# Attention of six blocks in 13 visits of TensorE with two units each, where 36 visits took one unit each

## The chip, the cores and the metric

The kernel runs on one core of a Trainium2 chip. The metric is the device time of one execution in microseconds (us). Three runs of the kernel before took 731.62, 733.33 and 733.63 us, a median of 733.33 us. A difference of less than about 0.3% (2.2 us) can't be told from none here.

## The reference

Two stages follow each other. The first is attention in chunks of 32 queries, each of which sees 8 memory keys, 16 keys to its left, its own 32 and 8 to its right; the second is a gated network with a norm ahead of it.

```python
q, k, v: (4 batches, 8 heads, 768 positions, 64)
for c in range(768 // 32):
    k_full = [mem_k, k[c*32-16 : c*32+32+8]]     # v_full likewise
    a = softmax(q_c @ k_full.T / 8)
    out[c] = a @ v_full
x  = out as (3072 tokens, 512)
xn = x / sqrt(mean(x*x) + 1e-6) * rms_g
y  = (silu(xn @ w_gate) * (xn @ w_val)) @ w_out   # 512 -> 1536 -> 512
```

## The kernel before

**Units and blocks.** The 3072 tokens are worked in eight blocks of 384. The attention of one block is four units, each of two heads (32 units in all, numbered 0 to 31). A unit runs through these steps: load q and k (`load_qk`) and v (`load_v`), transpose q and k on VectorE (`stage_t`, which ScalarE ends with two small copies inside k's tile), twelve score matmuls `s` (`stage_s`, L318), the maximum and the subtraction (`stage_m`: `mx` L330, `pe` L336), the exponential on ScalarE (`stage_e`, L341), three transposes of the weights on TensorE (`stage_p`: `pT`, L348), their copy out of PSUM in two halves, the first on ScalarE and the second on VectorE (`stage_c`, lines L227 and L230), twelve output matmuls `o` (`stage_o`, L368), and the division into the tile `x` (`stage_r`: L382, L386, L391). After a block's fourth unit `stage_n` norms `x`.

**The network.** Each block is worked through f = 0 to 11, twelve tiles of 128 hidden columns. For each f TensorE does twelve matmuls into `pg`, twelve into `pv` (L561, 384 columns each), and nine into the three `po` banks (L599, 512 columns) for the f before it. Every product is three matmuls on high and low parts in fp32r. From `pg` and `pv` ScalarE and VectorE make `t`, `hh` and `hl` (L568, L572, L575, L227, L584), which `po` takes 6 us later. At a block's end the next block's `x` is transposed on TensorE (`xT`, L440) and split into `xh` and `xl`.

**Order.** Up to 158 us a hand-written list (`ORDER`) sets everything: the attention of blocks 0 and 1 (units 0 to 7), the network of block 1, and the first five f of block 0. From there the main loop runs over six segments: block 0 from f = 5 on, then blocks 2 to 7. The gaps of a segment are numbered: after `pg` of its f-th tile comes gap 2f, after `pv` gap 2f+1 (counted from the segment's first f). In some of these gaps TensorE visits the attention of the next block. On TensorE the order of the program is kept. On the other engines a scheduler sets the order when the program is built, and each engine then works its own list strictly in that order; the attention steps have the higher priority.

**Visits before.** A block's attention takes seven steps, of which six have matmuls: visit n does `pT` of unit n-1, `s` of unit n and `o` of unit n-2. So what `o` needs was copied out of PSUM a visit earlier. All units of blocks 2 to 7 use one set of tiles: one for transposed q and weights (`qp`, in the place `A`), one for k and v (`kv`, in the place `B`), one landing tile for q (`qn`) and one for k (`kn`).

**PSUM.** `pg`, `pv` and the three `po` have one bank each. The other three banks are a ring (`psa`) which `pT`, `s`, `o`, `xT` and the scratch of the norm take in turn: a tile that is fourth in the ring waits until the first has been read out.

Of the kernel before, what the change touches and what calls it, by code (L numbers as in the profile page):

```python
# [8 lines left out]
F32 = mybir.dt.float32  # L9
# [10 lines left out]
CH = 32  # L20
# [16 lines left out]

FIRST = (1, 3, 5, 7, 9, 10, 11)
GAPS = 4
FA, FC = 3, 5  # L40
# [27 lines left out]
def tile_kernel(ctx: ExitStack, tc: tile.TileContext, q, k, v, mem_k, mem_v,  # L68
# [32 lines left out]
    pts = [None] + [early.tile([P, NT, 4, 2, CH], F32, name=f"pt{i}") for i in (1, 2)]  # L101
    zero = const.tile([P, 64], F32, name="zero")

# [13 lines left out]
    NE = NG * 2  # L117
    late_kv = {}
    KW, VW = (NC + 1) * KC, NJ * 2 * (D + 1)

    def late_attention():

        t = p1.tile([P, NKT * HT], F32, name="qp", tag="A")
        n = NC * 2 * CH
        qbs[0] = t[:, 0:n].rearrange("p (c s q) -> p c s q", c=NC, s=2)
        pts[0] = t[:, n:].rearrange("p (i a s q) -> p i a s q", i=NT, a=4, s=2)
        nc.vector.memset(t, 0.0)
        t = p1.tile([P, KW + VW], F32, name="kv", tag="B")
        late_kv["kw"] = t[:, 0:KW].rearrange("p (c k) -> p c k", k=KC)
        late_kv["vw"] = t[:, KW:].rearrange("p (j h d) -> p j h d", j=NJ, h=2)  # L130
    units = [(b, hf, g) for b in range(B) for hf in range(2) for g in range(NG)]
    st = {}

    def which(u):

        return 1 + u % 2 if u < NE else 0

    def unit_tile(u, shape, tag, n):

        if u < NE:  # L140
            return early.tile(shape, F32, name=f"{tag}{u}", tag=f"{tag}{u % n}")
        if tag in late_kv:
            return late_kv[tag]
        return p1.tile(shape, F32, name=f"{tag}{u}", tag=tag)

    def load_qk(u):
        b, hf, g = units[u]
        h0 = 2 * g
        t0 = hf * HT
        d = st.setdefault(u, {})  # L150
        if u < NE:

            k0 = t0 - hf * CH
            for n, src, r0, rows in (("q", q, t0, HT), ("k", k, k0, HT + CH)):
                x = d[n] = early.tile([P, 8, D], F32, name=f"{n}f{u}", tag=f"{n}f{u % NG}")[0:rows // 4]
                nc.sync.dma_start(out=x.rearrange("p (h r) d -> p h (r d)", h=2),
                                  in_=src[b, h0:h0 + 2, r0:r0 + rows].rearrange("h (p r) d -> p h (r d)", r=4))
            return

        d["q"] = qn = p1.tile([P, NC, CH], F32, name=f"qn{u}", tag="qn")  # L160
# [107 lines left out]
    def stage_q0(u, e="a"):  # L268
        d = st[u]
        qb = qbs[which(u)]  # L270
        q4 = split4(d["tq"], HT)
# [11 lines left out]
    def stage_ta(u):  # L283
        d = st[u]
        qb = qbs[which(u)]
        for hh in range(2):
# [22 lines left out]
    def stage_s(u):  # L309
        d = st[u]  # L310
        qb = qbs[which(u)]
        s = psum_a(f"s{u}")
# [42 lines left out]
    def stage_ch(u, hh, e):  # L355
        r = slice(64 * hh, 64 * hh + 64)
        t4 = st[u]["t"][:, 0:HT].rearrange("p (i a q) -> p i a q", i=NT, q=CH)
        copy(e, pts[which(u)][r, :, :, hh, :], t4[r])

    def stage_o(u):  # L360
        d = st[u]
        pt = pts[which(u)]
        o = psum_a(f"o{u}") if u >= NG else psum_m(f"o{1 + u % 2}", f"o{u}")
# [37 lines left out]
    def stage_n0(x):  # L401
        ss = p2.tile([P, 2, NT], F32, name="ss", tag="ss")
        squares(x, 0, NG - 1, ss[:, 0])
        return ss
# [4 lines left out]
    def stage_ny(ss):  # L409
        sr = p2.tile([P, NT], F32, name="sr", tag="sr")  # L410
        nc.vector.scalar_tensor_tensor(out=sr, in0=ss[:, 0], scalar=DM * 1e-6, in1=ss[:, 1], op0=ALU.add, op1=ALU.add)
# [239 lines left out]
    for cp in range(2):  # L651
        nc.scalar.dma_start(out=memV[64 * cp:64 * cp + NM], in_=mem_v[0].rearrange("h m d -> m h d"))
    first = const.tile([P, 1], F32, name="first")
    nc.scalar.activation(first, zero[:, 0:1], AF.Exp)
# [32 lines left out]

    def attn_visits(blk, x):


        us = list(range(blk * NG, (blk + 1) * NG))
        for n in range(NG + 2):
            with tc.high_priority():
                if 1 <= n <= NG:
                    stage_p(us[n - 1])
                if n < NG:
                    u = us[n]
                    stage_s(u)
                if n >= 2:
                    stage_o(us[n - 2])  # L700
                    stage_r(us[n - 2], x)
                if n < NG:
                    stage_m(u)
                    stage_e(u)
                if 1 <= n <= NG:
                    stage_c(us[n - 1])
                if n < NG and u + 1 < len(units):
                    stage_t(u + 1)
            if n >= 2 and us[n - 2] + 1 < len(units):
                load_v(us[n - 2] + 1)  # L710
            if n < NG and u + 2 < len(units):
                load_qk(u + 2)
            yield
        with tc.high_priority():
            stage_n(x)
        yield

# [137 lines left out]
    xs = xs01[0]  # L855
    nxt = 2
    for sg, (blk, f0) in enumerate(segments):
        po = [psm_o(i) for i in range(NT)] if sg else sp["po", 0]
        todo = iter(())
        if nxt < NBLK:  # L860
            x = new_x()
            todo = attn_visits(nxt, x)
            nxt += 1
        last = sg == len(segments) - 1
        gaps = 2 * (NF - f0)
        when = [n * (gaps - GAPS) // (NG + 1) for n in range(NG + 2)] + [gaps - GAPS + 1]
        if sg == 0:
            when = FIRST

        def visit(gap):  # L870
            for _ in range(when.count(gap)):
                next(todo, None)
        for f in range(f0, NF):
# [18 lines left out]
            else:  # L892
                for _ in todo:
                    pass
                prev = moe_h(g, vv)
                xs = split_x(x, out_, lambda: moe_out(NF - 1, prev, po))
        if sg == 0:
# [31 lines left out]
```

## Time and profile before

| what | value |
|---|---|
| runs | 731.62, 733.33, 733.63 us |
| span of the profiled execution | 729.8 us (its own run time is not recorded with it; the span leaves out 3.5 us of the median) |
| VectorE, ScalarE, GpSimd busy | 52%, 39%, 5% of the span |
| matmuls `pg` and `pv` | 384 of each of six kinds, 337 to 346 ns each |
| matmuls `po` | 285 of each of three kinds, 393 to 399 ns each |
| `s` and `o` of blocks 2 to 7 | 576 matmul records each, 228 and 224 ns |
| one main-loop segment of a whole block | 86.3 us (`po` groups at 302.71 and 388.96 us) |

A matmul's duration includes its way through the array, and the next starts before it has ended: `pg` and `pv` start 0.17 us apart, `po` 0.23 us. What a step costs TensorE is therefore read from starts, not from durations. An fp32 matmul of the attention shows as two records, so twelve `s` are listed as x24.

### The profile page before, as it was taken

Reading aid. Unit: us, or ns where it says so; the run is one execution under the profiler, and the core shown is the slowest. Engines: PE = TensorE matmul, PEld = TensorE weight load, DVE = VectorE, ACT = ScalarE, POOL = GpSimd, SP = SyncE. Lnnn points to the kernel's source line nnn. Section 1 sums busy time; section 2 is a strip of 40 time slices with the busy share of each in tenths; the row PEclk is TensorE's granted clock in tenths of the full one; section 3 lists DMA queues with packets and bytes.
Section 4 is the critical chain, followed back from the end, with each engine's and each line's share of the span. In section 5 each row is a group of like instructions: output and inputs, shape, how many; then the busy total and the mean of one; then the engine's idle time right before and its main releaser. Section 6 shows DMA issues by size and latency. Waiting matters only on the chain.

```text
span 729.8 us, 13052 instructions
## 1 busy us (share of the span) xinstructions
PE 715.1 (98%) x5136; PEld 656.6 (90%) x5136; DVE 380.0 (52%) x725; ACT 287.8 (39%) x600; POOL 36.4 (5%) x143
## 2 busy tenths in 40 slices
PE   8889999999999999999999999999999999999997
PEld 7778999999989999899999999989998999999996
DVE  4888999865645443444535353445434543332222
ACT  4899676643452323422333232432234222341112
POOL 3300000001000000000000000000000000000000
PEclk8999999999999999999999999999999999999999
DMA  8994563414412320122212123021311210010001
GB/s 173 203 259 141 173 202 116 132 37 102 85 37 68 55 50 22 62 46 42 43 38 66 23 45 61 20 66 31 66 29 34 64 32 20 20 44 0 1 1 43
DMA packets 143173, 50.20 MB, mean 69 GB/s; under 512 B 126984, under 2 KB 134536, under 8 KB 143112
## 3 DMA queue, kind: packets, MB, share of 16 engines
q1 hardware_dynamic: 139832, 44.49, 26.6%
q10 hardware_dynamic: 3280, 4.88, 1.8%
q8 instruction: 40, 0.66, 0.4%
q14 instruction: 21, 0.17, 0.1%
HBM read 43.06 MB, written 6.29 MB: 68 GB/s over the span
## 4 chain that ended last, share of the span: by engine, by line
PE 92%; ACT 3%; DMA 3%; DVE 1%; issue 0%; POOL 0%; ACTq 0%; SPq 0%; POOLq 0%
PE pv L561 28%; PE po L599 28%; PE pg L561 27%; PE s L318 3%; PE o L368 3%; PE xT L440 1%; PE pT L348 1%; DMA ws<-in_moe_w_val_dram 1%; DMA memV<-in_mem_v_dram 1%; DMA vw<-in_v_dram 1%; ACT junk L398 0%; ACT ws L508 0%; ACT pt L227 0%; DMA kv<-in_v_dram 0%; ACT qb L227 0%
## 5 line engine op out<-in xcount | busy, mean ns | idle before, releaser
L561 PE MATMUL pv<-xh,wh_v 128*128 128x384 f32 x384 | 132.8, 346 | 0.0
L561 PE MATMUL pg<-xh,wh_g 128*128 128x384 f32 x384 | 129.7, 338 | 0.7 <-DVE t L572 0.7
L561 PE MATMUL pv<-xh,wl_v 128*128 128x384 f32 x384 | 129.5, 337 | 0.6 <-DVE wl_v L532 0.6
L561 PE MATMUL pg<-xh,wl_g 128*128 128x384 f32 x384 | 129.5, 337 | 0.0
L561 PE MATMUL pg<-xl,wh_g 128*128 128x384 f32 x384 | 129.3, 337 | 0.0
L561 PE MATMUL pv<-xl,wh_v 128*128 128x384 f32 x384 | 129.3, 337 | 0.0
L572 DVE SCALAR_TENSOR_TENSOR t<-t,pg 128x384 f32<-128x384 f32 x96 | 53.1, 553 | 138.6 <-ACT t L568 138.5
L227 ACT CAST hh<-t 128x384 fp32r<-128x384 f32 x95 | 48.7, 512 | 174.9 <-PE po L599 165.3
L599 PE MATMUL po<-wh_o,hh 128*128 128x512 f32 x285 | 113.8, 399 | 0.3
L599 PE MATMUL po<-wh_o,hl 128*128 128x512 f32 x285 | 113.1, 397 | 0.0
L599 PE MATMUL po<-wl_o,hh 128*128 128x512 f32 x285 | 112.1, 393 | 0.0
L584 DVE TENSOR_TENSOR hl<-t,hh 128x384 fp32r<-128x384 f32 x95 | 52.9, 557 | 100.7 <-ACT hh L227 95.7
L568 ACT ACTIVATE t<-pg 128x384 f32<-128x384 f32 x96 | 47.2, 492 | 135.9 <-PE pg L561 130.8
L575 DVE TENSOR_TENSOR t<-t,pv 128x384 f32<-128x384 f32 x95 | 52.5, 552 | 64.9 <-PE pv L561 64.4
L561 PEld LDWEIGHTS pg<-xh,wh_g 128*128 128x128 f32 x384 | 72.1, 188 | 4.4 <-DVE t L572 0.9
L561 PEld LDWEIGHTS pg<-xl,wh_g 128*128 128x128 f32 x384 | 72.1, 188 | 3.6
L561 PEld LDWEIGHTS pv<-xh,wh_v 128*128 128x128 f32 x384 | 72.1, 188 | 2.4
L561 PEld LDWEIGHTS pv<-xh,wl_v 128*128 128x128 f32 x384 | 72.2, 188 | 0.9 <-DVE wl_v L532 0.9
L561 PEld LDWEIGHTS pv<-xl,wh_v 128*128 128x128 f32 x384 | 72.2, 188 | 0.3
L561 PEld LDWEIGHTS pg<-xh,wl_g 128*128 128x128 f32 x384 | 72.1, 188 | 0.0
L599 PEld LDWEIGHTS po<-wh_o,hl 128*128 128x128 f32 x285 | 53.5, 188 | 14.1 <-DVE hl L584 1.8
L599 PEld LDWEIGHTS po<-wh_o,hh 128*128 128x128 f32 x285 | 53.5, 188 | 10.0 <-ACT hh L227 1.7
(112 smaller groups left out, 772.9 us busy)
## 6 DMA issues: line engine op xcount, KB each, us to landing
kn<-in_k_dram SPq DMA_DIRECT2D x96, 52.0 KB
qn<-in_q_dram SPq DMA_DIRECT2D x96, 48.0 KB
out_dram<-ob ACTq DMA_DIRECT2D x18, 256.0 KB
ws<-in_moe_w_gate_dram SPq DMA_DIRECT2D x4, 1024.0 KB
ws<-in_moe_w_val_dram SPq DMA_DIRECT2D x4, 1024.0 KB
ws<-in_moe_w_out_dram SPq DMA_DIRECT2D x4, 1024.0 KB
kv<-in_v_dram SPq DMA_DIRECT2D x48, 84.0 KB
kv<-in_v_dram SPq DMA_DIRECT2D x48, 70.0 KB
```

The costliest lines, as they stand in the source:

```text
L227: return nc.scalar.copy(out, in_)
L318: on_pe(nc.tensor.matmul(s[64 * par:64 * par + 64, o:o + KC], lhsT=qb[:, c].rearrange("p s q -> p (s q)"), rhs=kw[:, c], start=True, stop= ...
L348: on_pe(nc.tensor.transpose(out=t[:, i * P:(i + 1) * P], in_=pe[:, i * P:(i + 1) * P], identity=ident))
L368: on_pe(nc.tensor.matmul(o[64 * par:64 * par + 64, c0:c0 + D + 1], lhsT=pt[:, i, 2 * par + hh].rearrange("p c q -> p (c q)"), rhs=d["v"][: ...
L440: on_pe(nc.tensor.transpose(out=t[:, i * P:(i + 1) * P], in_=tiles[i][:, kt * P:(kt + 1) * P], identity=ident))
L561: on_pe(nc.tensor.matmul(ps[:, 0:HT], lhsT=weight(a, n, f, kt), rhs=xs[c][:, kt], start=cnt == 0, stop=cnt == 3 * NKT - 1))
L568: nc.scalar.activation(t, g, AF.Tanh, scale=0.5)
L572: nc.vector.scalar_tensor_tensor(out=t, in0=t, scalar=1.0, in1=g, op0=ALU.add, op1=ALU.mult)
L575: nc.vector.tensor_tensor(out=t, in0=t, in1=vv, op=ALU.mult)
L584: nc.vector.tensor_tensor(out=hl, in0=t, in1=hh.bitcast(F32), op=ALU.subtract)
L599: on_pe(nc.tensor.matmul(po[i], lhsT=h[a][:, i * P:(i + 1) * P], rhs=weight(c, "o", f), start=f == 0 and n == 0, stop=f == NF - 1 and n == 2))
```

## The change

The units of blocks 2 to 7 are taken in pairs, twelve of them, in one chain over all segments (`late_steps`). A visit `v` does `pT` of both units of the pair before, `s` of both of the present one, and then `o` of both of the pair before, whose weights were copied in the same visit. Thirteen such visits replace the 36: three in the first segment (gaps 1, 5 and 10), and two in each later one (gaps 5 and 17). Steps `t` (transposes of a pair's second unit) and `n` (the norm) have gaps of their own and no matmuls.

Two units at a time need two sets of tiles. The second `qb` gets a place of its own, the second `pt` takes that of the weights' staging tile `wy`, and the second k and v tile, together with q's landing tile, that of `ws`. Both new tiles for q and weights are zeroed on VectorE. `zero` and `first` move to a pool that is given back early, and `ss` and `sr` have one buffer instead of two. For the very last f tile, `hh` and `hl` get tiles of their own, in the places `A` and `B`, which attention no longer uses by then.

```diff
-FIRST = (1, 3, 5, 7, 9, 10, 11)
-GAPS = 4
+VISITS = (((1, "v"), (3, "t"), (5, "v"), (7, "t"), (10, "v"), (11, "n"), (12, "t")),
+          ((5, "v"), (8, "t"), (17, "v"), (18, "n"), (20, "t")))
...
-        t = p1.tile([P, NKT * HT], F32, name="qp", tag="A")
...
+        t = p1.tile([P, NKT * HT], F32, name="qp0", tag="A")
+        late["qb", 0], late["pt", 0] = t[:, 0:NQ], t[:, NQ:]
         nc.vector.memset(t, 0.0)
...
+        for n, tag in (("qb", "qb"), ("pt", "wy")):
+            late[n, 1] = t = p1.tile([P, NQ], F32, name=f"{n}1", tag=tag)
+            nc.vector.memset(t, 0.0)
+        for i, tag in enumerate(("B", "ws")):
+            t = p1.tile([P, KW + VW + i * NC * CH], F32, name=f"kv{i}", tag=tag)
...
-    def attn_visits(blk, x):
...
-        us = list(range(blk * NG, (blk + 1) * NG))
-        for n in range(NG + 2):
...
-                if 1 <= n <= NG:
-                    stage_p(us[n - 1])
-                if n < NG:
-                    u = us[n]
-                    stage_s(u)
-                if n >= 2:
-                    stage_o(us[n - 2])
-                    stage_r(us[n - 2], x)
...
+    def late_steps():
...
+        pairs = [(u, u + 1) for u in range(NE, len(units), 2)]
+        for n in range(len(pairs) + 1):
+            old = pairs[n - 1] if n else ()
+            cur = pairs[n] if n < len(pairs) else ()
+            new = pairs[n + 1] if n + 1 < len(pairs) else ()
...
             with tc.high_priority():
...
+                for u in old:
+                    stage_p(u)
+                for u in old:
+                    stage_c(u)
+                for u in cur:
                     stage_s(u)
...
+                for u in cur[0:1]:
                     stage_m(u)
+                for u in old:
+                    stage_o(u)
+                for u in cur[1:2]:
+                    stage_m(u)
+                last_m = next(i for i in reversed(nc.cur_bb.bb.instructions) if i.engine == nc.vector.engine)
+                for u in cur:
                     stage_e(u)
...
+                for u in old:
+                    stage_r(u, x)
+                for u in new[0:1]:
+                    with tc.issue_after(last_m):
+                        stage_t(u)
+            for u in new[0:1]:
+                load_qk(u + 1)
+            for u in cur if n else ():
+                load_v(u)
+            yield "v"
+            if n and n % 2 == 0:
+                with tc.high_priority():
+                    stage_n(x)
+                yield "n"
+            if new:
+                with tc.high_priority():
+                    stage_t(new[1])
+                if n + 2 < len(pairs):
+                    load_qk(pairs[n + 2][0])
+            yield "t"
...
-        hh = p1.tile([P, HT], F32R, name="hh", tag="hh")
-        hl = p1.tile([P, HT], F32R, name="hl", tag="hl")
+        hh = p1.tile([P, HT], F32R, name="hh", tag="A")
+        hl = p1.tile([P, HT], F32R, name="hl", tag="B")
...
+    with tc.high_priority():
+        late_attention()
     load_qk(NE)
     with tc.high_priority():
-        late_attention()
         stage_t(NE)
     load_v(NE)
     load_qk(NE + 1)
+    with tc.high_priority():
+        stage_t(NE + 1)
+    load_v(NE + 1)
+    load_qk(NE + 2)
```

How the change moves the instructions is shown at three places. First TensorE at a visit in block 2's segment; `pT` are transposed weights, `s` scores, `o` outputs, and the last or first row is the network's matmul beside them. Before, in the segment's third visit:

```order
L561 MATMUL pg<-xh,wl_g_94 128x384
L348 MATMUL pT_2867<-ident,pe_2759 128x128 x3
L318 MATMUL s_2871<-kv,qp 64x64 x12
L368 MATMUL o_2884<-kv,qp 64x65 x12
L561 MATMUL pv<-xh,wh_v_95 128x384
```

and after, at gap 5:

```order
L573 MATMUL pv<-xh,wl_v_90 128x384
L360 MATMUL pT_2808<-ident,pe_2481 128x128 x3
L360 MATMUL pT_2812<-ident,pe_2511 128x128 x3
L330 MATMUL s_2820<-kv_1940,qp_1934 64x64 x12
L330 MATMUL s_2833<-kv_1941,qb_1936 64x64 x12
L380 MATMUL o_2850<-kv_1940,qp_1934 64x65 x12
L380 MATMUL o_2863<-kv_1941,pt_1938 64x65 x12
L611 MATMUL po_2701<-wh_o_91,hh 128x512
```

Six tiles now follow each other in the ring of three banks, and `o_2850` reads the weights that `pT_2808` of the same visit brought into PSUM.

Second VectorE at those two visits; `t` and `hl` belong to the network, `mx` and `pe` to `s`, the rows with `COPY` bring `pT` out of PSUM. Before:

```order
L572 SCALAR_TENSOR_TENSOR t_2954<-t_2954,pg_2854 128x384
L330 TENSOR_REDUCE mx14_2901<-s14_2871 128x6
L287 STREAM_TRANSPOSE qp_1944<-qn15_2771 64x12x32 x2
L292 STREAM_TRANSPOSE kv_1946<-kn15_2772 128x13x32
L336 TENSOR_TENSOR pe14_2903<-s14_2871,mx14_2901 128x384
L382 TENSOR_SCALAR r12_2897<-o12_2884 128x6
L230 COPY qp_1944<-pT13_2867 64x12x32
```

and after:

```order
L587 TENSOR_TENSOR t_2930<-t_2930,pv_2794 128x384
L242 COPY qp0_1934<-pT12_2808 64x12x32
L242 COPY pt1_1938<-pT13_2812 64x12x32
L342 TENSOR_REDUCE mx14_2846<-s14_2820 128x6
L348 TENSOR_TENSOR pe14_2848<-s14_2820,mx14_2846 128x384
L342 TENSOR_REDUCE mx15_2876<-s15_2833 128x6
L348 TENSOR_TENSOR pe15_2878<-s15_2833,mx15_2876 128x384
L299 STREAM_TRANSPOSE qp0_1934<-kv1_1941 64x12x32
```

The copies have moved from the end of the visit's work to its beginning, and the subtraction that ends the reading of the first scores stands fourth.

Third VectorE where the main loop starts, with the first units 8 and 9 (`qp`, `qb` are transposed q, `kv` transposed k; `kn8`, `kn9` the landing tiles). Before:

```order
L127 MEMSET qp_1944 128x1536
L292 STREAM_TRANSPOSE kv_1946<-kn8_1935 128x13x32
L584 TENSOR_TENSOR hl_1976<-t_1920,hh_1974 128x384
L287 STREAM_TRANSPOSE qp_1944<-qn8_1934 64x12x32 x2
L572 SCALAR_TENSOR_TENSOR t_2059<-t_2059,pg_1979 128x384
L575 TENSOR_TENSOR t_2059<-t_2059,pv_2010 128x384
L330 TENSOR_REDUCE mx8_2036<-s8_2023 128x6
L287 STREAM_TRANSPOSE qp_1944<-qn9_1964 64x12x32 x2
L584 TENSOR_TENSOR hl_2065<-t_2059,hh_2063 128x384
L292 STREAM_TRANSPOSE kv_1946<-kn9_1965 128x13x32
```

and after, behind the three MEMSET rows:

```order
L304 STREAM_TRANSPOSE kv0_1940<-kn8_1942 128x13x32
L596 TENSOR_TENSOR hl_2003<-t_1920,hh_2001 128x384
L299 STREAM_TRANSPOSE qp0_1934<-kv1_1941 64x12x32 x2
L584 SCALAR_TENSOR_TENSOR t_2102<-t_2102,pg_2005 128x384
L299 STREAM_TRANSPOSE qb1_1936<-kv1_1941 64x12x32
L587 TENSOR_TENSOR t_2102<-t_2102,pv_2036 128x384
L342 TENSOR_REDUCE mx8_2075<-s8_2049 128x6
L596 TENSOR_TENSOR hl_2108<-t_2102,hh_2106 128x384
L348 TENSOR_TENSOR pe8_2077<-s8_2049,mx8_2075 128x384
L299 STREAM_TRANSPOSE qb1_1936<-kv1_1941 64x12x32
L304 STREAM_TRANSPOSE kv1_1941<-kn9_1968 128x13x32
```

The transposes of unit 9 still stand behind the first scores' `mx8`, as before, but its scores are now in the first visit, right behind those of unit 8.

More of the change, by code (lines that the diff above doesn't have):

```diff
@@ L101, in tile_kernel @@
     pts = [None] + [early.tile([P, NT, 4, 2, CH], F32, name=f"pt{i}") for i in (1, 2)]
-    zero = const.tile([P, 64], F32, name="zero")
+    zero = early.tile([P, 64], F32, name="zero")
     pinned = []
@@ L141, in unit_tile @@
             return early.tile(shape, F32, name=f"{tag}{u}", tag=f"{tag}{u % n}")
-        if tag in late_kv:
-            return late_kv[tag]
-        return p1.tile(shape, F32, name=f"{tag}{u}", tag=tag)
+        if (tag, u % 2) in late:
+            return late[tag, u % 2]
+        return p1.tile(shape, F32, name=f"{tag}{u}", tag=f"{tag}{u % 2}")
     def load_qk(u):
@@ L158, in load_qk @@
             return
-        d["q"] = qn = p1.tile([P, NC, CH], F32, name=f"qn{u}", tag="qn")
+        d["q"] = qn = late["qn"]
         d["k"] = kn = p1.tile([P, NC + 1, CH], F32, name=f"kn{u}", tag="kn")
@@ L269, in stage_q0 @@
         d = st[u]
-        qb = qbs[which(u)]
+        qb = qb_of(u)
         q4 = split4(d["tq"], HT)
@@ L284, in stage_ta @@
         d = st[u]
-        qb = qbs[which(u)]
+        qb = qb_of(u)
         for hh in range(2):
@@ L310, in stage_s @@
         d = st[u]
-        qb = qbs[which(u)]
+        qb = qb_of(u)
         s = psum_a(f"s{u}")
@@ L357, in stage_ch @@
         t4 = st[u]["t"][:, 0:HT].rearrange("p (i a q) -> p i a q", i=NT, q=CH)
-        copy(e, pts[which(u)][r, :, :, hh, :], t4[r])
+        copy(e, pt_of(u)[r, :, :, hh, :], t4[r])
     def stage_o(u):
         d = st[u]
-        pt = pts[which(u)]
+        pt = pt_of(u)
         o = psum_a(f"o{u}") if u >= NG else psum_m(f"o{1 + u % 2}", f"o{u}")
@@ L401, in stage_n0 @@
     def stage_n0(x):
-        ss = p2.tile([P, 2, NT], F32, name="ss", tag="ss")
+        ss = p1.tile([P, 2, NT], F32, name="ss", tag="ss")
         squares(x, 0, NG - 1, ss[:, 0])
@@ L652, in tile_kernel @@
         nc.scalar.dma_start(out=memV[64 * cp:64 * cp + NM], in_=mem_v[0].rearrange("h m d -> m h d"))
-    first = const.tile([P, 1], F32, name="first")
+    first = early.tile([P, 1], F32, name="first")
     nc.scalar.activation(first, zero[:, 0:1], AF.Exp)
@@ L686, in new_x @@
         return p1.tile([P, NT, H, D], F32, name="x", tag="x")
-    def attn_visits(blk, x):
-        us = list(range(blk * NG, (blk + 1) * NG))
-        for n in range(NG + 2):
-            with tc.high_priority():
-                if 1 <= n <= NG:
-                    stage_p(us[n - 1])
-                if n < NG:
-                    u = us[n]
+    late_x = {}
+    def late_steps():
[4 more added lines that the diff above has]
+            new = pairs[n + 1] if n + 1 < len(pairs) else ()
+            for u in old[0:1]:
+                if u % NG == 0:
+                    late_x["x"] = new_x()
+            x = late_x.get("x")
+            with tc.high_priority():
+                for u in old:
[3 more added lines that the diff above has]
+                for u in cur:
@@ L698, in attn_visits @@
                     stage_s(u)
-                if n >= 2:
-                    stage_o(us[n - 2])
-                    stage_r(us[n - 2], x)
-                if n < NG:
+                for u in cur[0:1]:
                     stage_m(u)
-                    stage_e(u)
[L705 to L716, printed above, removed]
+                for u in old:
[4 more added lines that the diff above has]
+                for u in cur:
+                    stage_e(u)
+                for u in old:
+                    stage_r(u, x)
@@ L855, in tile_kernel @@
     xs = xs01[0]
-    nxt = 2
+    todo = late_steps()
     for sg, (blk, f0) in enumerate(segments):
         po = [psm_o(i) for i in range(NT)] if sg else sp["po", 0]
[L859 to L863, printed above, removed]
         last = sg == len(segments) - 1
[L865 to L868, printed above, removed]
+        steps = {} if last else dict(VISITS[min(sg, 1)])
         def visit(gap):
-            for _ in range(when.count(gap)):
-                next(todo, None)
+            if gap in steps and next(todo, None) not in (steps[gap], None):
+                raise AssertionError(gap)
         for f in range(f0, NF):
@@ L892, in tile_kernel @@
             else:
-                for _ in todo:
-                    pass
                 prev = moe_h(g, vv)
-                xs = split_x(x, out_, lambda: moe_out(NF - 1, prev, po))
+                xs = split_x(late_x["x"], out_, lambda: moe_out(NF - 1, prev, po))
         if sg == 0:
```

23 lines of the change are left out of this document (13 added, 10 removed).

## The prediction

> **What bounds the kernel now.** I read the page first: busy shares and the chain of work that ended last.
>
> ```profile
> span 729.8 us, 13052 instructions
> PE 715.1 (98%) x5136; PEld 656.6 (90%) x5136; DVE 380.0 (52%) x725; ACT 287.8 (39%) x600; POOL 36.4 (5%) x143
> PE 92%; ACT 3%; DMA 3%; DVE 1%; issue 0%; POOL 0%; ACTq 0%; SPq 0%; POOLq 0%
> ```
>
> TensorE is the bound. The other engines matter only where TensorE asks for something that isn't there yet. The view of the waits, from 64 us on for TensorE and from 160 us on for its weight loads, holds a single entry that touches the visits:
>
> ```profile
> PE o L368 <- DMA kv<-in_v_dram: 0.8, 1, 0.8
> ```
> ```profile
> PEld o L368 <- DMA kv<-in_v_dram: 0.3, 1, 0.3
> ```
>
> So 1.1 us in all, once, in block 2's segment, where `o` waits for a load of v. All the other visits run without a wait, and what they cost is work and switching. The timeline of TensorE prices them. Columns are start, duration, engine and line; two visits with the network's matmuls around them:
>
> ```profile
> 306.95 0.34 PE L561 MATMUL pg<-xh,wl_g 128*128 128x384 f32 x1
> 307.22 0.97 PE L318 MATMUL s<-kv,qp 128*64 128x64 f32 x24
> 308.12 0.45 PE L561 MATMUL pv<-xh,wh_v 128*128 128x384 f32 x1
> 308.40 0.34 PE L561 MATMUL pv<-xl,wh_v 128*128 128x384 f32 x1
> ```
> ```profile
> 332.44 0.34 PE L561 MATMUL pg<-xh,wl_g 128*128 128x384 f32 x1
> 332.62 0.49 PE L348 MATMUL pT<-ident,pe 128*128 128x128 f32 x3
> 333.03 0.97 PE L318 MATMUL s<-kv,qp 128*64 128x64 f32 x24
> 333.78 0.92 PE L368 MATMUL o<-kv,qp 128*64 128x65 f32 x24
> 334.63 0.44 PE L561 MATMUL pv<-xh,wh_v 128*128 128x384 f32 x1
> 334.91 0.34 PE L561 MATMUL pv<-xl,wh_v 128*128 128x384 f32 x1
> 335.08 0.34 PE L561 MATMUL pv<-xh,wl_v 128*128 128x384 f32 x1
> ```
>
> Undisturbed, the network's matmuls start 0.17 us apart (334.91 to 335.08). From the last one ahead of a visit to the second behind it the first visit has 1.45 us; less two such steps, 0.35, it costs **1.10**. The second has 2.47 and costs **2.12**. Twelve `s` take 0.75 (333.03 to 333.78). So 0.35 of the first visit is no work of its own: the price of leaving the network and coming back. A `pT` and an `o` together add 2.12 - 1.10 = 1.02, of which the `pT` is about a third (0.41 with the switch ahead of `s`) and `o` 0.70.
>
> **The change part by part.**
>
> *Fewer visits.* The units and their matmuls stay, 24 of each. 36 visits become 13, and 23 x 0.35 = **8.05** falls away. The one wait for v goes as well if v comes a visit early, as the order of the loads gives it: **1.1**. Together -9.2.
>
> *Waits inside a visit.* Six tiles pass a ring of three banks. By the order shown above, the second `s` needs the bank of the first `pT`, so it waits for VectorE's copy of it; the first `o` waits for the second copy, and the second `o` for the subtraction that ends the reading of the first scores. Before, all of these had several us, up to the next visit. What they last, from a visit of before and from a place with `mx` and `pe` back to back:
>
> ```profile
> 172.17 0.49 PE L348 MATMUL pT<-ident,pe 128*128 128x128 f32 x3
> ```
> ```profile
> 172.69 0.47 ACT L227 COPY qp<-pT 64x384 f32<-64x384 f32 x1 [1.01 <-PE pT L348]
> 173.20 0.56 DVE L230 COPY qp<-pT 64x384 f32<-64x384 f32 x1 [0.28 <-ACT qp L227]
> ```
> ```profile
> 12.29 0.56 DVE L330 TENSOR_REDUCE mx<-s 128x6 f32<-128x384 f32 x1 [3.20 <-PE s L318]
> 12.88 0.56 DVE L336 TENSOR_TENSOR pe<-s,mx 128x384 f32<-128x384 f32 x1
> ```
>
> VectorE's half waits for ScalarE's half: the bracket at 173.20 says so. Count from the first `pT` of a visit. The first copy starts on VectorE at 173.20 - 172.17 = 1.03 and ends at 1.59. TensorE has done both `pT` at 0.75 and the first `s` at 1.50, and goes on at 1.63: **0.13** lost. VectorE's second copy ends at 2.18, and the first `o`, asked for at 2.38, finds it done. `mx` starts at 2.21, `pe` 0.59 later at 2.80, ends at 3.34. The second `o` is asked for at 2.38 + 0.70 = 3.08 and goes at 3.38: **0.30** lost. That is 0.43 in each of ten whole visits, 4.3. In the visit at gap 10, which follows `pg`, a product of `t` stands ahead of the first copy and I count 0.16 more, 0.59. The last visit has no `s` between `pT` and `o`: the first copy, at 1.63, is asked for at 0.75: 0.9. In sum **+5.8**. It can't be below 0; it is 9 if every step is 0.15 later. Behind the waiting matmuls stands the whole network on TensorE, so each wait counts in full.
>
> *Starting again after a wait.* A matmul behind a wait may lose a little more than the wait:
>
> ```profile
> 61.10 0.44 PE L561 MATMUL pv<-xh,wl_v 128*128 128x384 f32 x1 [0.60 <-DVE wl_v L532]
> 61.38 0.34 PE L561 MATMUL pv<-xh,wh_v 128*128 128x384 f32 x1
> ```
>
> 0.28 to the next where 0.17 is usual, 0.11 lost. With 22 waits this is 0 to 2.4; small matmuls already start slowly in a visit, so I take 0.04 each: **+0.9**. The Trainium skill, TensorE: Matmul & The Clock Gate, in the section on the array's architecture in Part 1, says that TensorE's queue can pull weight loads ahead of matmuls in flight. By that a wait would hide the next load and this term would be 0, the sum 0.9 lower; the two rows, with 0.11 lost, speak against it.
>
> *The first visit.* Units 8 and 9 now have their scores in one visit. Before, unit 9's came with the next visit. The order of VectorE shown above puts unit 9's transposes where they were, behind `mx8`, which needs unit 8's scores:
>
> ```profile
> 166.93 0.97 PE L318 MATMUL s<-kv,qp 128*64 128x64 f32 x24
> ```
> ```profile
> 167.93 0.56 DVE L330 TENSOR_REDUCE mx<-s 128x6 f32<-128x384 f32 x1 [0.34 <-PE s L318]
> 168.41 1.17 DVE L287 STREAM_TRANSPOSE qp<-qn 64x384 f32<-64x384 f32 x2
> 169.60 0.56 DVE L584 TENSOR_TENSOR hl<-t,hh 128x384 fp32r<-128x384 f32 x1
> 170.08 0.60 DVE L292 STREAM_TRANSPOSE kv<-kn 128x416 f32<-128x416 f32 x1
> ```
> ```profile
> 170.96 0.27 ACT L301 COPY kv<-kv 128x96 f32<-128x96 f32 x1
> ```
>
> TensorE has done unit 8's scores at 166.93 + 0.75 = 167.68. On VectorE after `mx8` (to 168.40) now stand `hl` (0.48 by its row), `pe8`, the second half of q's transposes and k's, with half an us or a little more each: k's ends at 170.5, ScalarE's two copies follow as at 170.96, and unit 9's scores can start at 171.1. TensorE waits **3.4** us. Moving the first half ahead of `t` saved one half transpose, `pe8` took its time. The two additional memsets on VectorE, each of half the first one's columns, delay unit 8's transposes, but these had ended long before unit 8's scores began, so I count them at nothing. The loads of unit 9 go out behind v of both units and behind unit 8's transposes on SP's queue, as far as 166.6; if the last ones land late, the wait grows, to 4.9 by my count. Less than 3.4 isn't possible in this order.
>
> *The clock.* Does a wait of that length cost more? The trace has one that is comparable, at the start; then windows of 1 us, in which the column behind GpSimd's share is the granted clock:
>
> ```profile
> 11.31 0.94 PE L318 MATMUL s<-kw,qb 128*64 128x64 f32 x24 [2.45 <-POOL kw L221]
> ```
> ```profile
> 12.00:13.00 1.00, 1.00 (x18) 0.93 (x13) 0.67 (x2) 0.08 (x1) 0.44 (x3) 0.96 1.00 290
> 13.00:14.00 1.00, 1.00 (x9) 1.00 (x8) 0.55 (x2) 0.65 (x2) 0.18 (x1) 0.50 1.20 166
> ...
> 19.00:20.00 1.00, 1.00 (x15) 0.72 (x15) 0.13 (x1) 0.64 (x2) 0.00 (x0) 0.62 1.11 259
> ```
>
> TensorE stood still for 2.45 us, and from 12.92 to 19.76 it had half the clock: 6.8 us, 3.4 of them lost if it is busy throughout. Matmuls were sparse there, dense work follows here, so one half of that length is as likely: 1.7. I take **+2.2**, between 0 and 3.4. The same page, Part 1, on the clock gate, says that half clock follows a whole idle window of about 3.4 us and ends after one busy window. By that, one window is lost, 1.7, and only if the wait fills a window; the trace agrees on the half, but its drop came after only 2.45 us, and it lasted two such lengths.
>
> *The norm in block 2's segment.* After gap 10 the norm of block 2 and its `xT` follow closely:
>
> ```profile
> L398 ACT ACTIVATE junk<-x 128x384 f32<-128x384 f32 x24 | 11.9, 494 | 0.5
> L398 ACT ACTIVATE junk<-x 128x128 f32<-128x128 f32 x24 | 6.8, 282 | 3.3 <-DVE x L391 2.7
> L398 ACT ACTIVATION_READ_ACCUMULATOR junk<-x 128x1 f32 x48 | 9.0, 188 | 0.0
> L412 POOL TENSOR_TENSOR sr<-sr,mhalf 128x3 f32<-128x3 f32 x8 | 7.8, 969 | 59.4 <-DVE sr L411 59.4
> ```
>
> Six squares with their reads are 3 x (0.49 + 0.19) + 3 x (0.28 + 0.19) = 3.4, the power on GpSimd 0.97, then a transpose of k (0.60) and the scaling on VectorE. I put the end of the division at 7.9 us into the visit, an estimate from two exponentials, the copies and six divisions of half a us each behind the last `s`; from there this reaches 13.4 with a scaling of 0.5, and TensorE, which has 36 steps of 0.17 us and 9 of 0.23 of the network behind a visit of 4.5, needs it at 12.8. I take **+0.6**, from 0 to 1.5. In later segments some 25 us of network lie between, so nothing.
>
> *The tail.* With tiles of their own the last `hh` needn't wait for the last `po` to read the old one:
>
> ```profile
> 723.06 0.40 PE L599 MATMUL po<-wh_o,hl 128*128 128x512 f32 x1
> ```
> ```profile
> 723.61 0.50 PE L627 MATMUL po<-wh_o,hh 128*128 128x512 f32 x1 [0.15 <-ACT hh L621]
> ```
>
> A `po` step is 0.23, so it could follow at 723.29 and not 723.61: **-0.4** with the restart.
>
> *Sum.* -9.2 + 5.8 + 0.9 + 3.4 + 2.2 + 0.6 - 0.4 = **+3.3**. The profiled execution has no time of its own on record; its span of 729.8 leaves 3.5 us to the median of the three runs, 733.33, on which I put the sum: **736.5** us, rounded. With the bounds of the forecast's unknowns (restart, norm, clock from 1.7 to 3.4) it is 735 to 738.5.
>
> **Rivals.**
>
> *The wait comes, the clock stays.* For it: the one drop that the trace shows came where matmuls were sparse on both sides of the idle stretch; here they are dense. The sum loses 2.2: 734.3, no change that can be seen.
>
> *The waits inside the visits aren't there, and it is faster.* It is one mechanism: copies and subtraction are through before TensorE asks. The point that decides is 1.50 us after the first `pT` for the first copy and 3.08 for the subtraction; my count misses them by 0.13 and 0.30 only, so 0.15 less a step would do. Then 5.8 and 0.9 fall, and if the clock holds too, -9.2 + 3.4 + 0.6 - 0.4 = -5.6: 727.7; with half of the waits left, 731.0. Against it: the bracket at 173.20 shows that the two halves of a copy follow each other.
>
> *More waits.* Unit 9's loads are late (+1.5), and in the four visits at gap 17 of the middle segments VectorE stands in front of a k that hasn't landed, with `t` of the network queued behind it (0 to 0.9 each, say 0.6): +3.9, 740.4.
>
> **How the numbers follow.** Forecast 0.40, clock stays 0.25, no waits inside 0.20, more waits 0.15. Three runs of before spread over 2 us, so within 0.3% (2.2 us) nothing can be told from no change: the bounds are 731.1 and 735.5. Faster takes nearly all of the third case: 0.19. Same takes the second and the forecast's lower edge, 0.35; slower the rest, 0.46. The range leaves out half of the third and half of the last case: 729.5 to 740.0.
>
> **What would show it.** Right: one wait of `s` of 3.4 us near 167 us for ScalarE's copies in k, half clock for one or two stretches of 3.4 us behind it, `s` waiting about 0.13 for VectorE's copy and `o` about 0.30 for `pe` in each later visit, and full visits of 3.9 + 0.43 us. Wrong: a first visit without a wait, for then unit 9 was transposed earlier; a granted clock of 1.00 behind it; visits under 4.0; or waits of the network's matmuls (for `t`, `hh` or `xT`) that weren't there before.

## The result and the profile after

The changed kernel takes 739.50 us (five runs, 738.62 to 740.05) where the kernel before takes 733.29 (five runs): +6.2 us. The ratio is 1.0091, with a 95% interval from 1.0078 to 1.0104. It is slower, as forecast, but by about twice the +3.2 us of the prediction. The profiled execution has a span of 737.7 us and took 739.50 itself, so the span leaves out 1.8 us. By the same 1.8 the profiled execution of before, with its 729.8, took about 731.6, an estimate that puts it at the fast end of its five runs; so the two spans differ by more than the medians. Its page, the lines that answer to those of before:

```profile
span 737.7 us, 13168 instructions
PE 715.5 (97%) x5136; PEld 660.2 (89%) x5136; DVE 378.3 (51%) x727; ACT 283.5 (38%) x600; POOL 36.0 (5%) x143
PE 88%; ACT 4%; DVE 3%; DMA 2%; issue 1%; SPq 0%; POOL 0%; ACTq 0%; DVEq 0%; POOLq 0%
```

TensorE is still the bound, but its share of the chain has fallen from 92% to 88%: other engines now stand in it. The view of the waits of TensorE, from 64 us on, names the largest:

```profile
PE s L330 <- ACT kv L313: 3.4, 1, 3.4
PE o L380 <- issue: 0.9, 1, 0.9
PE s L330 <- DVE qp L242: 0.3, 1, 0.3
PE pg L573 <- DVE t L584: 0.2, 1, 0.2
```

The 0.9 is in the last visit, which has no `s` between `pT` and `o`. The waits inside the other visits hardly appear here: a listed matmul ends later than the next one could start, so a short wait leaves no idle time. The starts on the timeline show them; TensorE, ScalarE and VectorE in the visit at 242.05 us:

```profile
242.05 0.82 PE L360 MATMUL pT<-ident,pe 128*128 128x128 f32 x6
...
242.80 0.97 PE L330 MATMUL s<-kv,qp 128*64 128x64 f32 x24
242.96 0.47 ACT L239 COPY pt<-pT 64x384 f32<-64x384 f32 x1
243.08 0.56 DVE L242 COPY qp<-pT 64x384 f32<-64x384 f32 x1 [0.28 <-ACT qp L239]
243.56 0.55 DVE L242 COPY pt<-pT 64x384 f32<-64x384 f32 x1
243.79 0.94 PE L330 MATMUL s<-kv,qb 128*64 128x64 f32 x24
...
244.51 0.92 PE L380 MATMUL o<-kv,qp 128*64 128x65 f32 x24
244.74 0.56 DVE L348 TENSOR_TENSOR pe<-s,mx 128x384 f32<-128x384 f32 x1
...
245.51 0.93 PE L380 MATMUL o<-kv,pt 128*64 128x65 f32 x24
```

The second `s` could start at 243.55 (0.75 behind the first) and starts at 243.79, when VectorE's copy of the first weights has ended at 243.64. The second `o` could start at 245.21 and starts at 245.51, when `pe`, which frees the first scores' bank, has ended at 245.30. The whole visit costs 4.42 us; without the waits the prediction counted 3.9.

The first visit and the clock behind it, TensorE first and then windows of 1 us (the number behind GpSimd's share is the granted clock):

```profile
168.66 0.97 PE L330 MATMUL s<-kv,qp 128*64 128x64 f32 x24
172.99 1.60 PE L330 MATMUL s<-kv,qb 128*64 128x64 f32 x24 [3.37 <-ACT kv L313]
174.53 0.69 PE L573 MATMUL pg<-xh,wh_g 128*128 128x384 f32 x1
175.01 0.52 PE L573 MATMUL pg<-xl,wh_g 128*128 128x384 f32 x1
175.33 0.52 PE L573 MATMUL pg<-xh,wl_g 128*128 128x384 f32 x1
```
```profile
172.00:173.00 1.00, 0.01 (x1) 0.01 (x1) 0.40 (x1) 0.51 (x2) 0.00 (x0) 0.63 0.24 38
173.00:174.00 1.00, 1.00 (x18) 1.00 (x20) 0.00 (x0) 0.00 (x0) 0.32 (x2) 0.50 0.48 77
...
179.00:180.00 1.00, 1.00 (x7) 1.00 (x6) 0.91 (x2) 0.32 (x1) 0.00 (x0) 0.96 0.61 99
```

Unit 9's scores wait 3.37 us for ScalarE's copies in k. The clock falls to half at 172.3 and is back at 179.1. In between twelve `s` take 1.54 us instead of 0.75, and the network's matmuls start 0.32 us apart instead of 0.17.

The drop at the start of the kernel, from which the prediction had read 6.8 us, is there too, but shorter:

```profile
11.00:12.00 1.00, 0.42 (x11) 0.45 (x13) 0.00 (x0) 0.98 (x4) 0.64 (x5) 0.92 0.97 242
15.00:16.00 1.00, 0.94 (x10) 0.73 (x9) 0.34 (x1) 0.54 (x2) 0.00 (x0) 0.88 0.54 99
```

With half the clock between them, these two windows put the drop from 11.8 to 15.2 us: 3.4 us, where the profile of before has 6.8.

### The profile page after: what moved, and what is told of

It reads as the page before. It is cut to its first block, busy times and chain, and to the rows that moved or that the text cites. A ratio compares the mean times of both kernels' runs of the same rounds, so it can differ in the third digit from the quotient of the medians.

```text
span 737.7 us, 13168 instructions
## 1 busy us (share of the span) xinstructions
PE 715.5 (97%) x5136; PEld 660.2 (89%) x5136; DVE 378.3 (51%) x727; ACT 283.5 (38%) x600; POOL 36.0 (5%) x143
## 4 chain that ended last, share of the span: by engine, by line
PE 88%; ACT 4%; DVE 3%; DMA 2%; issue 1%; SPq 0%; POOL 0%; ACTq 0%; DVEq 0%; POOLq 0%
PE po L611 27%; PE pg L573 27%; PE pv L573 27%; PE s L330 3%; PE o L380 3%; PE xT L452 1%; DMA ws<-in_moe_w_val_dram 1%; PE pT L360 1%; DMA memV<-in_mem_v_dram 1%; ACT pt L239 0%; ACT junk L410 0%; ACT ws L520 0%; ACT qb L239 0%; DVE kw L242 0%; ACT wy L521 0%
## 5 line engine op out<-in xcount | busy, mean ns | idle before, releaser
L573 PE MATMUL pv<-xh,wh_v 128*128 128x384 f32 x384 | 130.0, 339 | 0.0
```

The source lines that it names most:

```text
L573: on_pe(nc.tensor.matmul(ps[:, 0:HT], lhsT=weight(a, n, f, kt), rhs=xs[c][:, kt], start=cnt == 0, stop=cnt == 3 * NKT - 1))
```

## The experiments

Each run is compared with runs of the kernel before on the same chip, made beside it; the medians of these were 732.3 to 733.4 us. A median set against that of the kernel after comes from another set of runs, so a difference of about 1 us between the two shows nothing by itself. Against its own set of before, the kernel after is at +6.2 us, the split visit at +1.2, the two fills at +5.7 and +5.2, the copies at +6.1 and +3.1, the 32 bytes at +3.7. What was expected is quoted as it stood ahead of each run.

**The kernel before once more.** No edit.

> The kernel before, unchanged. Its first network matmul started at 51.80 us in the profile before and at 52.71 us in the profile after, and in the last stretch without visits the network took 0.28 us longer over 76 us after. Theory A (both are spread between executions): another profile of the kernel before shows a first pg anywhere from 51.8 to 52.8 us and the last 76 us up to 0.3 us longer, span 729.5 to 732. Theory B (the change costs this): 51.8 again and the same rate, span within 0.3 of 729.8.

732.65 us, ratio 0.9996 (0.9984 to 1.0008); span 731.3. The first `pg` came at 53.78 us, two us later than in the other profile of the same kernel and one later than in that of after: the start varies between executions, and nothing is read from it. The rate of the network doesn't vary. In the stretch without visits at the end, the first `pg` and the last group of `po` on TensorE's timeline, here and then in the profile of the kernel after:

```profile
651.50 0.34 PE L561 MATMUL pg<-xh,wh_g 128*128 128x384 f32 x1
...
722.64 0.40 PE L599 MATMUL po<-wh_o,hh 128*128 128x512 f32 x1
```
```profile
658.12 0.34 PE L573 MATMUL pg<-xh,wh_g 128*128 128x384 f32 x1
...
729.55 0.39 PE L611 MATMUL po<-wh_o,hh 128*128 128x512 f32 x1
```

71.14 us against 71.43, for the same matmuls in the same order. The other profile of before gives 71.13. So for the start theory A held, with a spread wider than it gave, and for the rate theory B: the change slows the network itself by 0.42%. That had no place in the prediction.

**Unit 9's scores in a visit of their own.**

```diff
-VISITS = (((1, "v"), (3, "t"), (5, "v"),
+VISITS = (((1, "v"), (3, "s"), (4, "t"), (6, "v"),
...
-                for u in cur:
+                for u in cur if n else cur[0:1]:
                     stage_s(u)
                 for u in cur[0:1]:
                     stage_m(u)
+            if not n:
+                yield "v"
+            with tc.high_priority():
+                for u in () if n else cur[1:2]:
+                    stage_s(u)
```

> The scores of unit 9 stand at gap 3, in a visit of their own, and the next visit at gap 6. Theory A (the first visit is what makes the change slow: a wait of 3.4 us and half clock for 6.8 us behind it): both go, the two visits cost 1.10 each, less 6.3 us: 733 us, granted clock 1.00 from 160 us on. Rival (the half clock comes from something else in this stretch, such as the loads, or the wait moves to the next visit, where unit 11 isn't ready): the half clock stays or a wait of 2 to 3 us appears at gap 6, 736 to 739 us.

733.89 us, ratio 1.0025 (1.0009 to 1.0040): 5.6 us less than the kernel after. Windows of this kernel over the stretch in question:

```profile
165.00:185.00 20.00, 19.87 (x140) 17.73 (x139) 13.19 (x25) 6.86 (x16) 1.17 (x6) 1.00 0.66 129
```

The clock is 1.00 throughout, and the two visits cost 1.1 us each. The first visit cost more than any other single place of the change, wait and clock together.

**Filling the wait.** Unit 8's score matmuls are repeated into the bank of unit 9's scores, which then overwrite them; first 50, then 28.

```diff
                 for u in cur:
+                    if not n and u % 2:
+                        fill(u - 1, 50)
                     stage_s(u)
```

> 50 matmuls of unit 8's scores are repeated into the bank of unit 9's scores before these, about 3.1 us of work (0.0625 us each) in the wait of 3.37 us; nothing else changes. Theory A (the half clock follows from TensorE's standing still): the wait shrinks to about 0.3 us, the clock stays at 1.00, and the time falls by what the half clock cost, 3.1 us, to 736.4. Rival (the wait alone costs, the half clock is a matter of load or chance): 739.5, half clock still there.

738.40 us, ratio 1.0078 (1.0058 to 1.0098). The clock stayed at 1.00, but the fill was mis-sized: all matmuls into one place of one bank take 0.117 us each, 5.83 in all, 2.5 more than the wait. The 6.27 us of the first visit became 7.63. By the starts on TensorE this loses 1.4, and the matmuls behind it, at full clock, win 1.9; the median itself is too near that of the kernel after to show it.

> The kernel after with 28 repeated matmuls in the first visit's wait; in the run with 50 one took 0.117 us, so these fill 3.3 of the 3.37 us. Theory A (half clock follows from standing still): granted clock 1.00 throughout, the first visit stays at 5.3 to 5.6 us (1.85 of work and the wait), and the matmuls behind it start 0.17 us apart: less 3.1 us, 736.4. Rival (less than the whole wait must be filled with dense work for the clock to hold, or the fill delays VectorE's or ScalarE's part): half clock again, 739.5, or a visit of over 6 us.

737.54 us, ratio 1.0074 (1.0053 to 1.0096). TensorE's timeline of this kernel and the window with the wait:

```profile
169.64 3.43 PE L327 MATMUL s<-kv,qp 128*64 128x64 f32 x56
173.97 0.97 PE L339 MATMUL s<-kv,qb 128*64 128x64 f32 x24 [0.90 <-ACT kv L313]
174.86 0.44 PE L582 MATMUL pg<-xh,wh_g 128*128 128x384 f32 x1
175.15 0.34 PE L582 MATMUL pg<-xl,wh_g 128*128 128x384 f32 x1
175.32 0.34 PE L582 MATMUL pg<-xh,wl_g 128*128 128x384 f32 x1
```
```profile
173.00:174.00 1.00, 0.10 (x4) 0.03 (x2) 0.37 (x1) 0.51 (x2) 0.40 (x3) 1.00 0.26 41
```

With TensorE standing still for 0.9 us instead of 3.37 the clock holds, and the steps behind are 0.17. Unit 9 came 0.75 us later here (5.08 us behind unit 8's scores, 4.33 in the kernel after), which takes most of what is missing from the 3.1 us expected: the medians differ by 2.0, and by 1.0 when each is set against its own before. The profiled execution also has two waits further on that the profile of after hasn't: 0.4 of `s` for a copy of GpSimd in the next visit, and 1.0 of block 2's `xT` for the norm of `x`. So the time isn't accounted for to the end. That the half clock follows from standing still is shown by the clock in both fills, 1.00 where four profiles with the whole wait (the kernel after, two of the runs with other copies, the 32 bytes) all have half clock for 6.8 us; what it costs is better read from the profile of after.

**Copies.** Three divisions of the four copy halves of a visit. First the first unit's weights whole on VectorE, the second's on ScalarE:

```diff
-                    stage_c(u)
+                    stage_ch(u, 0, "da"[u % 2])
+                    stage_ch(u, 1, "da"[u % 2])
```

> The pair's first weights are copied whole by VectorE, the second whole by ScalarE, so that neither waits for the other's half. Theory A (the second o waits because the subtraction stands third behind two copy halves on VectorE): VectorE's copy ends at about 1.62 as before, mx and pe follow at once, pe ends at 2.8 and the second o, asked for at 3.17, does not wait: visits fall from 4.42 to about 4.13 us, 2.9 us in all, 736.6. The second s still waits 0.24. Rival (the waits are set by something else, such as the semaphore's way or ScalarE): visits stay at 4.3 to 4.4, 739.

738.79 us, ratio 1.0075 (1.0053 to 1.0097), which can't be told from the kernel after; visits of 4.31, 0.11 less. The second `o` doesn't wait any more, but VectorE's two halves, behind `t`, end later than one behind ScalarE's did:

```profile
243.75 1.12 DVE L242 COPY qp<-pT 64x384 f32<-64x384 f32 x2
```

They end 1.80 us into the visit instead of 1.59, and the second `s` goes at 1.94 instead of 1.74. The last visit, which has no `s` between, grew from 3.36 to 3.66. Then all four halves on ScalarE (`"a"` for both):

> The kernel after with all four copy halves of a visit on ScalarE. From the trace after, one half follows the other there 0.37 us later and takes 0.47. Theory A (the waits inside the visits come from the copies and the subtraction alone): the first copy ends at 0.52 + 0.37 + 0.47 = 1.36, the second at 2.10, VectorE does mx and pe from 1.6 to 2.75; the second s (asked for at 1.50), the first o (2.2) and the second (2.95) find all done, and a visit falls from 4.42 to 3.9 to 4.0 us: ten visits, less 4 to 5 us, 735.0. Rival (the waits move on, to ScalarE's exponentials and to t and hh of the network, which queue behind the copies): visits of 4.2 and more, or new waits of pg or po, 738 to 739.

736.50 us, ratio 1.0045 (1.0029 to 1.0061); visits of 4.23, 0.19 less: under half of what theory A gave. The timeline of this kernel:

```profile
241.95 0.96 ACT L239 COPY qp<-pT 64x384 f32<-64x384 f32 x2 [1.92 <-PE pT L360]
242.93 0.96 ACT L239 COPY pt<-pT 64x384 f32<-64x384 f32 x2
```

Two halves take 0.96 here, not 0.84, so the second copy ends 2.47 us into the visit that began at 241.42, and the first `o` waits for it until 2.57. This pointed to the third division, ScalarE for the first weights, VectorE and ScalarE for the halves of the second. It was run on top of the combined kernel below.

**An unused tile of 32 bytes.** No instruction changes, on any engine; only the addresses of the tiles behind it in SBUF.

```diff
+    const.tile([P, 8], F32, name="pad")
     rg = const.tile([P, NKT], F32, name="rg")
```

> The kernel after with an unused tile of 32 bytes ahead of the others in SBUF; no instruction changes. x, xh, xl, hh, hl and t, which the kernel before has at addresses of 32 modulo 64 and the kernel after at 0 modulo 64, are at 32 again. Both profiles of the kernel before show 71.13 and 71.14 us for the last stretch without visits (from the 35th last group of network matmuls to the last), all four profiles with the layout of after 71.43 or 71.44. Theory P (placement: the network reads its operands more slowly at these addresses, 0.42%): 71.13 again, and over the network's 570 us from 160 us on 2.4 us less: 737.1. Rival (the longer stretch has another cause, such as the program's length): 71.43 stays, 739.5.

737.06 us, ratio 1.0054 (1.0036 to 1.0072): 2.4 us less than the kernel after. The stretch:

```profile
656.40 0.34 PE L574 MATMUL pg<-xh,wh_g 128*128 128x384 f32 x1
...
727.49 0.40 PE L612 MATMUL po<-wh_o,hh 128*128 128x512 f32 x1
```

71.09 us. The same 32 bytes in the kernel before:

> The kernel before with the same 32 bytes: its tiles go to 0 modulo 64; no instruction changes. Theory P: the last stretch takes 71.43 us, and the time rises by 2.4 us to 735.1. Rival: 71.13, 732.7.

731.32 us, ratio 0.9979 (0.9967 to 0.9991): faster, where theory P as I had put it said slower.

```profile
651.12 0.33 PE L562 MATMUL pg<-xh,wh_g 128*128 128x384 f32 x1
...
722.04 0.40 PE L600 MATMUL po<-wh_o,hh 128*128 128x512 f32 x1
```

70.92 us. So where the tiles lie does set the rate of the network (both runs changed nothing else, and both moved it), but the rule of 32 against 0 modulo 64 is wrong. A second rule was put to 64 bytes in the kernel before:

> The kernel before with 64 unused bytes ahead; no instruction changes. Rule 1 (tiles at 32 modulo 64 against 0 modulo 64, which the run of before with 32 bytes has already contradicted): as the kernel before, 71.13 us for the last stretch, 733. Rule 2 (pg and pv take 2.11 us where both xh, xl and the weights lie in the upper half of 128 bytes, modulo 128 at 64 or 96, and 2.08 elsewhere, as in the four layouts seen; po takes 2.05 where hh, hl and w_out both lie at 96): xh and xl go to 32 modulo 128, hh and hl to 96, so pg and pv take 2.08 at every f and po 2.05 from the sixth f on: 70.75 us for the stretch and 729.5 to 730.5 in all.

732.86 us, ratio 1.0001 (0.9989 to 1.0013), and a stretch of 71.06: rule 2 is wrong as well.

**Together.** The split first visit, the copies on ScalarE and the 32 bytes:

> The split first visit, all copies on ScalarE and the 32 bytes together. If the three causes are separate and add up: 739.5 less 5.6 (first visit, as measured) less 4.5 (copies) less 2.4 (placement) = 727.0, faster than the kernel before by 5.7 us, 0.8%. If the copies on ScalarE only move the wait: 731 to 732, no difference from before. If placement does nothing: 729.4.

729.10 us, ratio 0.9945 (0.9928 to 0.9963). The clock was 1.00, the visits 4.23. Measured against the kernel before this is 4.3 us less, where the sum gave 5.7; most of the difference is the copies, which brought 3 of the 4.5 us counted for them. With the third division:

```diff
-                    stage_ch(u, 0, "a")
-                    stage_ch(u, 1, "a")
+                    stage_ch(u, 0, "ad"[u % 2])
+                    stage_ch(u, 1, "a")
```

> The combined kernel with other copies: the first weights of a pair whole by ScalarE, of the second the lower half by VectorE and the upper by ScalarE. In the combined kernel the first o went at 2.57 because ScalarE's four halves of 0.47 follow each other to 2.45. Theory A: the second copy ends at 2.05, mx and pe run on VectorE from 1.6 to 2.75, nothing is late but the second s by 0.09, a visit takes 4.0 to 4.1 us where it took 4.23: less 2 us, 727.1. Rival (VectorE's half and mx delay each other, or ScalarE's half comes after the exponential): 4.2 or more, 729.

727.19 us, ratio 0.9928 (0.9901 to 0.9955), the fastest of all. A visit of this kernel:

```profile
234.21 0.82 PE L361 MATMUL pT<-ident,pe 128*128 128x128 f32 x6
234.73 0.96 ACT L240 COPY qp<-pT 64x384 f32<-64x384 f32 x2 [1.92 <-PE pT L361]
234.95 0.97 PE L331 MATMUL s<-kv,qp 128*64 128x64 f32 x24
235.06 0.55 DVE L243 COPY pt<-pT 64x384 f32<-64x384 f32 x1
235.65 0.47 ACT L240 COPY pt<-pT 64x384 f32<-64x384 f32 x1
235.79 0.94 PE L331 MATMUL s<-kv,qb 128*64 128x64 f32 x24
236.51 0.92 PE L381 MATMUL o<-kv,qp 128*64 128x65 f32 x24
236.56 0.56 DVE L349 TENSOR_TENSOR pe<-s,mx 128x384 f32<-128x384 f32 x1
237.33 0.93 PE L381 MATMUL o<-kv,pt 128*64 128x65 f32 x24
```

VectorE and ScalarE copy side by side; the second weights are out at 236.12, before the first `o` asks at 236.51, and a visit costs 4.08. That is 0.34 less than in the kernel after, where 0.5 was above the work. Last, the same kernel with its small constants in fewer tiles, which puts x, xh, xl, hh, hl and the last weights at multiples of 128 bytes:

> The kernel of the run before this one with two pairs of small constants in one tile each and without the 32 bytes, so that x, xh, xl, hh, hl and the last two groups of weights lie at 0 modulo 128; nothing else changes. Rule 2: pg and pv take 2.08 at every f, the last stretch 70.7 to 70.95 us instead of 71.10, the whole 1.5 to 3 us less: 724 to 725.5. Rival (only some other relation of the addresses matters): 71.1 or more, 727 or more.

729.24 us, ratio 0.9960 (0.9949 to 0.9972), 2.1 us more than without, and the slowest stretch of all, 71.49 us. What relation of the addresses counts is open.

## Why the prediction was right in its direction and wrong in its size

The views give each term of the sum. Visits are priced as in the prediction, from the network's last start ahead of them to its second behind them. By this the 36 visits of before cost 56.5 us, and the 13 of after 58.4, of which 1.05 are half clock.

| term | predicted | measured |
|---|---|---|
| fewer visits, no wait for v | -9.2 | -9.2 (as counted; only its sum with the next term is measured, by 56.5 against 58.4) |
| waits inside visits, starting again | +6.7 | +6.7: behind the first, nine visits of 4.42 and others of 4.31, 4.68 and 3.36 are 52.1 us; 45.4 of work, from the visits of before, and these 6.7 are 52.1 |
| first visit | +3.4 | +3.37 |
| half clock | +2.2 | +2.9 |
| norm of block 2 | +0.6 | 0: `xT` costs 0.98 there as in the other blocks; the last part of `x` was ready 0.2 us before TensorE loaded it |
| memsets in the first segment | 0 | +0.4 |
| `t` late behind visits at gap 17 | 0 (in a rival) | +0.7 |
| tail | -0.4 | -0.4 |
| the network's own steps | none | +2.1 |

The measured column sums to 6.6. The two profiles differ by 7.9 us in span; 1.3 of them were there when the main loop began (the same `pg` at 160.54 and 161.85 us), from a start that varies, and 6.6 are left. The median moved by 6.2.

**What was right.** The mechanism of the large terms: fewer visits gain 9.2, and the waits give most of it back. The copies and the subtraction were late where the count from the order said (0.24 and 0.30 measured, 0.13 and 0.30 predicted, the rest in the term for starting again). The wait of 3.4 us and the half clock were there, so the rival in which the clock stays is out, as is the faster one: its condition was a copy and a subtraction 0.15 us earlier. The copies on VectorE and ScalarE showed that these waits are most of what a visit costs above its work: the best division took away 0.34 of 0.5 us, and each moved them as its own timeline says. The rival with more waits named 740.4, nearer to 739.50 than the forecast, but that is luck: of its 3.9 us only the 0.7 for `t` came.

**The step that failed** is one that the sum hasn't got. It prices visits, waits and moved work, and takes the steps between the network's matmuls, 0.17 and 0.23 us, as the same in both kernels. The part on the change speaks of tiles that get new places, and I costed new places at nothing without saying so. They made the network 0.42% slower, 0.30 us in 71.13. The main loop has some 508 us of them (737.7 less 162 before it, 58 of visits and 10 of `xT`), so this is 2.1 us; the 32 bytes took it away again (739.50 to 737.06, and 71.09 us for the stretch) without moving one instruction. The steps of the whole main loop, those beside visits and waits left out, say the same: the matmuls of one f tile take 6.30 us on average, 6.28 before and 6.28 with the 32 bytes. No row of before could have priced it, since each profile shows one placement. The range reached 740.0 for other reasons and so still held the result; the forecast's own bound of 738.5 didn't.

**Terms that were mis-sized.** The half clock lasted 6.8 us (172.3 to 179.1), the length of the row of before (12.92 to 19.76). I took 2.2 as a middle between one half of that length and both, arguing that dense work would end it sooner. It didn't: 2.9. That the two lengths agree is luck, though: at the start of the kernel the drop lasted 3.4 us in the profile of after, and between none and 10.2 in the others, so one row of one execution couldn't size this term. The Trainium skill, TensorE: Matmul & The Clock Gate, Part 1, on the clock gate, says that half clock ends after one busy window of about 3.4 us. The trace doesn't contradict it: of the two such lengths, the first began with 0.7 us of standing still (172.3 to 172.99), and only the second was dense throughout. The norm's term, 0 in this profile, hung on 0.2 us; in the run with 28 repeated matmuls `xT` waited 1.0 us for it. The memsets delayed unit 8's transposes without harm, as said, but `hl` of the network stood behind them too. VectorE's `hl` and TensorE's third `po` in the kernel after show it:

```profile
164.16 0.51 DVE L596 TENSOR_TENSOR hl<-t,hh 128x384 fp32r<-128x384 f32 x1
```
```profile
164.20 0.40 PE L611 MATMUL po<-wl_o,hh 128*128 128x512 f32 x1
164.73 0.50 PE L611 MATMUL po<-wh_o,hl 128*128 128x512 f32 x1
```

0.53 instead of 0.23, and 0.1 more behind it. And `pg` waited for `t` some 13 us behind the visit at gap 17 in two segments, 0.4 and 0.1, with 0.1 more for starting again each time. VectorE stands in front of loads there, with `t` queued behind; the first of the two:

```profile
295.77 0.57 DVE L299 STREAM_TRANSPOSE qb<-kv 64x384 f32<-64x384 f32 x1 [1.68 <-DMA kv<-in_q_dram]
296.45 0.61 DVE L304 STREAM_TRANSPOSE kv<-kn 128x416 f32<-128x416 f32 x1
296.98 0.52 DVE L584 SCALAR_TENSOR_TENSOR t<-t,pg 128x384 f32<-128x384 f32 x1
```

That is the mechanism of the rival with more waits (with q's load here, and k's beside it in the second segment), for which I had put 0.6 in each of four segments; such a wait was also on the prediction's own list of signs that it is wrong. In the run with the split first visit the same two places had 0.1 and 0.7. What decides when these loads land was not tried.

## What to carry to other kernels

Merging visits to save a fixed price (0.35 us each here) also shortens the way from a producer to its reader, so write down for each buffer in the ring when it is asked for and when the other engines are through; that count was exact to 0.1 us a visit, and the cure was to let two engines copy side by side. A wait of TensorE of some 3 us in the midst of dense work costs nearly twice its length through the clock (3.4 and 2.9 us here); split the work rather than wait. When a kernel that is 98% TensorE moves tiles, measure a stretch that the change doesn't touch: if its rate moves at full clock, try another placement; a pad of 32 bytes was worth 2.4 us here, a third of what the change cost.

## What the runs showed of the hardware

- **Placement.** The same 71 us of matmuls took 70.92, 71.06, 71.09, 71.13, 71.43 and 71.49 us in six placements of their tiles in SBUF. Where a placement was profiled more than once, the value came back to 0.02 us, also with other work in the visits (71.43 and 71.44 in six kernels, 71.09 and 71.10 in three). Two rules in the addresses, modulo 64 and modulo 128, were tried and fell.
- **The clock.** It fell to half in a wait of 3.37 us with dense work on both sides, for 6.8 us; a wait of 0.90 in the same place left it at 1.00. At the start of the kernel, where TensorE stands still for 2.0 to 3.1 us between sparse matmuls, the same work had half clock for 6.8 us in the profile of before, 3.4 in that of after, 10.2 in two others and not at all in three: there it varies from one execution to the next.
- **Repeated matmuls into one place.** Score matmuls that write the same 64 partitions and columns again and again took 0.117 us each, where the twelve of a unit, which take different columns and both halves of the partitions in turn, take 0.0625 each (twelve in 0.75). Whether the columns or the partitions count was not tried.
- **Two copies on ScalarE.** Halves of different tiles started 0.38 us apart (242.58 and 242.96 in the kernel after), halves of the same tile took 0.96 for the two, so the second starts 0.48 behind the first (the runs with the first weights' copies on ScalarE).
